# Top-k attention with an exact-GELU MLP on one core: larger halves before the reciprocal, one product copied before exponentials, two more items turned by squares

## The chip, the cores and the metric

The kernel runs on one core of a Trainium2 chip. The core has five engines that work side by side and meet through semaphores: TensorE (PE in the profile; its weight loads are listed apart as PEld), VectorE (DVE), ScalarE (ACT), GpSimd (POOL) and SyncE (SP), which here only issues DMAs. Each engine runs its own instructions strictly in the order in which the kernel wrote them; one that waits holds up all that stand behind it on the same engine. The metric is the device time of one execution in microseconds, as a median of several.

## The reference

All data are float32. The first half is attention that keeps the 32 largest scores of each row; the second is an MLP with an exact GELU on its output.

```python
B, H, S, D = 8, 8, 576, 64
scores = (q @ k.T) / sqrt(D)                     # per batch and head, 576 x 576
kth    = 32nd largest score of each row
scores = where(scores >= kth, scores, -1e9)
attn   = exp(scores - max); attn = attn / (sum(attn) + 1e-9)
x      = (attn @ v) reshaped to 4608 tokens x 512
out    = gelu(x @ w_in) @ w_out                  # w_in 512 x 2048, w_out 2048 x 512
```

## The kernel before, in words

**Items.** Attention is cut into 144 items. An item is a pair of heads of one batch and a tile of 128 query rows; its scores fill an SBUF tile `s` of 128 partitions by 2 x 576. The last 64 rows of the 576 are handled in items of their own, two head pairs together. A batch has 18 items, 16 of whole tiles and 2 of the last rows. Two batches, 36 items, repeat the same pattern; `RINGS` is 36, and "a ring" below means such a stretch. An item's place in its ring is its number modulo 36.

**The loop.** One loop over n writes the instructions of all engines by hand; it is the only thing that sets their order (`manual_schedule`). In step n it writes the scores of items n+2 and n+3 together when n is even (`scores`, L408 on TensorE, copied to `s` by ScalarE at L416, the keys of the last 64 columns at L381), the top-k of item n (`top_k`), mask and exponentials of item n-1 (`select` L538 and `softmax` L550 on ScalarE), the transposes of item n-2 (`transposes`), and the product with v of items n-3 or n-4 (`attend`, L742). Between these stand small pieces of the MLP (`mlp`): the first product (L811), GELU on ScalarE (L827) and the second product, which saves a multiplication by sums of blocks (L965 and L967; the sums of blocks are formed on GpSimd at L848 to L851). These pieces fill TensorE while attention waits for other engines.

**The top-k.** The row of 576 scores is split in two halves. Most items are "paired": VectorE writes the elementwise maximum of the halves into a tile `lists` (`larger`, L443), GpSimd writes their sum as integers (`sum_up`, L468) and later subtracts the maximum (`smaller`, L476), which leaves the smaller halves. VectorE then takes eight maxima at a time with MAX8 (L504) and MATCH_REPLACE8 (L507), first in the larger halves alone, then in all. Items 18 to 27 are not paired. After the last MAX8 of step n VectorE takes the reciprocal of item n-1's row sums (`inverse`, L525), for which GpSimd has added 1e-9 to the sums (`add_small`, L531). Behind them GpSimd writes the threshold and the exponent's bias of item n (`threshold`, L518 and L519), multiplies item n-1 by the reciprocals (`normalise`, L573) and starts `sum_up` for item n+2. `larger(n + 1)` is written at the head of step n, so on VectorE it stands right behind the reciprocal of step n-1. The tile `lists` has two buffers.

**From `s` to the product.** The product needs the probabilities with keys on the partitions. There are two ways. The first is on TensorE: one transpose for the last columns (L657) and eight for the others (L671) into PSUM, and ScalarE copies both to the tile `pt` (L660, L686). The second, "by squares" (`squared`), is off TensorE: VectorE transposes blocks of 32 by 32 inside `s` (`square_p`, L605, written in the middle of the next but one top-k), SP writes the result to DRAM (`write_p`, L615, four DMAs) and reads it back turned into `pt` (`read_p`, L625, four DMAs). Even items go by squares, and of the odd ones those whose place is in `LATER`; the latter are called "moved". The product of a moved item is written one step later, by `mids`, its PSUM tile is of the tag `pr`, which the transposes L671 and the second of two score tiles use too, and it is copied to `xT` by ScalarE (L747). The copy follows directly on the product in ScalarE's order; for a moved item it stands between the two exponentials of step n.

Of the kernel before, what the change touches and what calls it, by code (L numbers as in the profile page):

```python
# [14 lines left out]
def kernel(  # L15
# [19 lines left out]
    nc = tc.nc  # L35
    f32, i32, u32 = mybir.dt.float32, mybir.dt.int32, mybir.dt.uint32
    bf16, i16, u16 = mybir.dt.bfloat16, mybir.dt.int16, mybir.dt.uint16
    AF = mybir.ActivationFunctionType
    ALU = mybir.AluOpType

    B, H, S, D = q.shape
    P = 128
# [20 lines left out]
    work = ctx.enter_context(tc.tile_pool(name="work", bufs=2))  # L63
# [46 lines left out]
    def flush():  # L110
        held[0] = False
        while late_issues:
            late_issues.pop(0)()
        late_issues.extend(later)
        later.clear()
# [142 lines left out]
    for b in range(B):  # L258
# [4 lines left out]
        last = [(b * NP + p, NM) for p in range(0, NP, 2)]  # L263
# [13 lines left out]
    few = [False]  # L277
# [151 lines left out]
    lists_of = {}  # L429
    HS = S // 2  # L430

    def paired(i):

        return PAIRED <= i < N and i not in SINGLE

    def halves_of(i):
        s = S_of[i].rearrange("p (e h n) -> p e h n", e=2, h=2)
        return s[:, :, 0], s[:, :, 1]

    def larger(i):  # L440

        if paired(i):
            nc.vector.tensor_tensor(lists_of[i][:, :, 0], *halves_of(i), op=ALU.max)  # L443

    def into_of(i):

        if i < 2 and i not in into_lists:
            into_lists[i] = work.tile([P, 2, 2, HS], f32, tag="pt", bufs=1, name="into")
        return into_lists.get(i, lists_of[i])
# [3 lines left out]
    def first_lists():  # L453
# [6 lines left out]
        nc.gpsimd.tensor_tensor(both, a.bitcast(i32), top, op=ALU.subtract)  # L460
        nc.gpsimd.tensor_tensor(both, both, b.bitcast(i32), op=ALU.add)

    def sum_up(i):

        if paired(i):
            lists_of[i] = t = work.tile([P, 2, 2, HS], f32, tag="lists", name="lists")
            a, b = halves_of(i)
            nc.gpsimd.tensor_tensor(  # L468
                t[:, :, 1].bitcast(i32), a.bitcast(i32), b.bitcast(i32), op=ALU.add
            )  # L470
# [7 lines left out]
    def top_k(i, last, middle):  # L478


        stat_of[i] = st = {
            "first": work.tile([P, 2, 8], f32, tag="first", name="first"),
        }
        stat = work.tile([P, 4, 2], f32, tag="stat", name="stat")
        st.update((n, stat[:, x]) for x, n in enumerate(("neg", "bias", "den", "rden")))
        top = work.tile([P, 2, 16], f32, tag="top", bufs=1, name="top")
        into = [st["first"]] + [
            top[:, :, 8:16] if r == TOPK // 8 - 1 else top[:, :, 0:8] for r in range(1, TOPK // 8)
        ]
        if paired(i):  # L490
            t = lists_of[i]
            u = into_of(i)
            both = u.rearrange("p e h n -> p e (h n)")
            rounds = [(t[:, :, 0], u[:, :, 0]), (u[:, :, 0], u[:, :, 0])]
            rounds = [(*(rounds[r] if 16 * r < TOPK else (both, both)), x) for r, x in enumerate(into)]
        else:
            s = S_of[i].rearrange("p (e n) -> p e n", e=2)
            t = work.tile([P, 2, S], f32, tag="lists", name="rest")
            rounds = [(s if r == 0 else t, t, x) for r, x in enumerate(into)]
        for r, (src, dst, x) in enumerate(rounds):  # L500
            if 16 * r == TOPK:
                middle()
            for e in range(2):
                nc.vector.max(x[:, e], src[:, e])  # L504
            if r < len(rounds) - 1:
                for e in range(2):
                    nc.vector.match_replace(dst[:, e], x[:, e], src[:, e], LOWEST)  # L507
            if r == len(rounds) - 1:
                last()

        st["kth"] = top[:, :, 15]
# [9 lines left out]
    def inverse(i):  # L521
        if i < 0 or i >= N:
            return
        st = stat_of[i]
        nc.vector.reciprocal(st["rden"], st["den"])  # L525
# [17 lines left out]
    def softmax(i, e):  # L543

        if i < 0 or i >= N:
            return
        st, s = stat_of[i], row(i, e)
        if (i, e) not in selected:
            select(i, e)
        nc.scalar.activation(  # L550
            s, s, func=AF.Exp, bias=st["bias"][:, e : e + 1], scale=1.0,
            accum_out=st["den"][:, e : e + 1],
        )
# [23 lines left out]
    def squared(i):  # L577

        if not SINGLE.stop - 2 < i < N - 2:
            return False  # L580
        if items[i][1] == NM:
            return i % RINGS != RINGS // 2 - 1
        return moved(i) or (i % 2 == 0 and i % RINGS != 12)

    LATER = (3, 13, 25)

    def moved(i):

        return RINGS <= i < N - 8 and i % RINGS in LATER

    def delayed(i):

        return squared(i) and items[i][1] == NM
# [4 lines left out]
    RINGS = 2 * len(items) // B  # L598
    turned = {}

    def square_p(i):

        if squared(i):
            s = S_of[i]
            nc.vector.transpose(s, s)  # L605

    def write_p(i):

        if squared(i):
            turned[i] = d = dram.tile([SQ, NJ + NM, P // SQ, P], f32, tag="turned", name="turned")  # L610
            s = S_of.pop(i).rearrange("p (x j) -> p x j", j=SQ)
            d = d.rearrange("i c k n -> i (c k) n")
            for a in range(P // SQ):
                rows = slice(a * SQ, (a + 1) * SQ)
                nc.sync.dma_start(out=d[:, :, rows], in_=s[rows])  # L615
# [498 lines left out]
    def mlp(n):  # L1114
        for _ in range(n):
            if done[0] >= len(pieces) or pieces[done[0]][0] > ready[0] or left[0] == 0:
                return
            pieces[done[0]][1]()
            done[0] += 1
            left[0] -= 1  # L1120
            if eager[0]:
                run_gelus()
                run_small(9)
# [33 lines left out]
    for pair in range(2):  # L1157
        for piece in transpose_qk(pair, pair == 0):
            piece()
        if pair == 0:  # L1160
            scores(0)
            first_lists()
            scores(1)
            sum_up(1)
# [28 lines left out]
    starts_next = [x + 1 for x in starts]  # L1193
    sums_in = {START + 8 + j: j for j in range(FT // 2)}
    ahead = N + 4
    for n in range(ahead):

        held[0] = n < N and squared(n - 2)
        mid = [i for i in (n - 5, n - 4) if delayed(i) and n % 2 and (i % 2 or i in starts)]
        if moved(n - 4):  # L1200
            mid = [n - 4]
# [9 lines left out]
        def mids():  # L1211
            attend(mid.pop(0))
            if not mid:
                copy_x()
                read_p(n - 3)
                issue_soon()
# [7 lines left out]
        if n > 0:  # L1224
            larger(n + 1)
# [57 lines left out]
            softmax(n - 1, 1)  # L1283
        if few[0]:
            room = ODD if n % 2 else 0
            if mid and mid[0] in starts_next:
                mlp(1)
                mids()
                room -= 1
            if n % 2 or not ahead_of_x:  # L1290
                softmax(n - 1, 0)
            if mid:
                mlp(1)
                mids()
                room -= 1
            if n % 2 and ahead_of_x:
                softmax(n - 1, 1)
            mlp(room)
# [35 lines left out]
        mlp(left[0])  # L1334
        run_gelus()
        if n < N:
            top_k(n, lambda: inverse(n - 1), lambda: square_p(n - 2))
            write_p(n - 2)
            flush()
            if n == 0:  # L1340
                larger(1)
        else:
            inverse(n - 1)
        threshold(n)
        if n == 0:
            smaller(1)
        normalise(n - 1)
        sum_up(n + 2)
        if n in sums_in:
            weight_sums(sums_in[n])  # L1350
# [56 lines left out]
```

## Time and profile before

| | us |
|---|---|
| median of 3 runs (1465.57 to 1466.32) | 1465.61 |
| the profiled execution | 1466.12 |
| its span, first to last instruction | 1464.0 |
| TensorE busy | 1444.8 |
| VectorE busy | 1323.7 |
| GpSimd busy | 1138.0 |
| ScalarE busy | 1060.0 |

Rows of the timeline give the start in us from the span's beginning, the duration in us, the engine, the line of the kernel, the operation, the tiles as out<-in, the shapes, and how many were merged into the row. Square brackets hold the engine's idle time before it and who ended that. A matmul in float32 shows as two records. Rows of the groups give the count, busy us, the mean in ns, and the idle time before. Rows of the waits give the waiting instruction, the one that ended the wait, us in total, how often, and the longest. Rows of the windows give the window, its length, and each engine's busy us with its number of instructions (PE, PEld, DVE, ACT, POOL, as far as they are shown), then the granted share of TensorE's clock, the DMA share and GB/s. Rows of the DMAs end with the KB of one and the median us from issue to landing.

### The profile page before, as it was taken

To read this page: it belongs to the slowest core of one execution; us is meant where nothing else is said; L and a number is where in the kernel's file an instruction comes from. 1 tells how busy PE (TensorE), PEld (TensorE's weight loads), DVE (VectorE), ACT (ScalarE), POOL (GpSimd) and SP (SyncE) were. 2 spreads that over 40 slices of the span, in tenths; PEclk is the share of its full clock that TensorE was granted. 3 is DMA by queue.
4 is the path that set the end of the run, shared out by engine and by line. 5 is a ranking of instruction groups with operands and counts; after the bars stand their busy time and mean duration, and the time that the engine had idled before them with its cause. 6 is when DMAs were issued, how large, how long until landed. Compare 5 with 4: busy or idle time off the path is not lost. (4 is left out here: it accounts for less than half of the span.)

```text
span 1464.0 us, 26591 instructions
## 1 busy us (share of the span) xinstructions
PE 1444.8 (99%) x8639; PEld 1126.5 (77%) x8639; DVE 1323.7 (90%) x3337; ACT 1060.0 (72%) x1887; POOL 1138.0 (78%) x1290
## 2 busy tenths in 40 slices
PE   8999999999999999999999999999999999999999
PEld 6776677877777777787777778787777777787887
DVE  7999899999999999999999999999999999999701
ACT  7999977876777777767777777776776767677620
POOL 6877667877897879877898878887788887978632
PEclk9999999999999999999999999999999999999999
DMA  7524310045454446455454365455555443643300
GB/s 193 152 87 124 85 48 1 16 96 99 90 113 89 84 91 141 82 112 113 96 100 95 61 116 115 89 114 112 98 100 110 86 84 78 128 99 75 65 15 15
DMA packets 580043, 134.13 MB, mean 92 GB/s; under 512 B 494881, under 2 KB 571457, under 8 KB 579905
## 3 DMA queue, kind: packets, MB, share of 16 engines
q1 hardware_dynamic: 578640, 132.01, 42.6%
q8 instruction: 68, 1.11, 0.3%
q14 instruction: 71, 0.57, 0.1%
q10 hardware_dynamic: 1200, 0.39, 0.1%
q0 software_dynamic: 64, 0.03, 0.0%
HBM read 84.01 MB, written 48.37 MB: 90 GB/s over the span
## 5 line engine op out<-in xcount | busy, mean ns | idle before, releaser
L811 PE MATMUL h_ps<-xT,w_in_sb 128*128 128x256 f32 (+1 forms) x2560 | 533.2, 361 | 0.0
L811 PEld LDWEIGHTS h_ps<-xT,w_in_sb 128*128 128x128 f32 x2560 | 438.2, 190 | 70.3 <-issue 11.3
L504 DVE MAX8 top<-lists 128x8 f32<-128x576 f32 (+1 forms) x792 | 475.0, 638 | 0.0
L507 DVE MATCH_REPLACE8 lists<-top,lists 128x288 f32<-128x288 f32 (+1 forms) x528 | 307.4, 587 | 0.0
L538 ACT ACTIVATE s<-s,stat 128x576 f32<-128x576 f32 x288 | 217.8, 778 | 113.4 <-POOL stat L518 113.2
L573 POOL TENSOR_TENSOR s<-s,stat 128x1152 f32<-128x1152 f32 x135 | 286.3, 2121 | 0.3 <-DVE stat L525 0.3
L550 ACT ACTIVATE s<-s,stat 128x576 f32<-128x576 f32 x288 | 223.8, 780 | 7.6
L468 POOL TENSOR_TENSOR lists<-s 128x576 int32<-128x576 int32 x133 | 189.9, 1427 | 0.0
L476 POOL TENSOR_TENSOR lists<-lists 128x576 int32<-128x576 int32 x132 | 186.1, 1410 | 3.1
L742 PE MATMUL o<-pt,raw_v 128*64 128x256 f32 x1280 | 152.9, 384 | 1.5 <-issue 0.6
L416 ACT ACTIVATE s<-s_ps 128x1024 f32<-128x1024 f32 x127 | 125.0, 1032 | 39.6 <-PE s_ps L408 39.5
L531 POOL TENSOR_SCALAR stat<-stat 128x2 f32<-128x2 f32 x144 | 31.4, 218 | 153.7 <-ACT s L550 147.2
L742 PEld LDWEIGHTS o<-pt,raw_v 128*64 128x64 f32 x1280 | 87.4, 136 | 81.9 <-issue 38.9
L967 PE MATMUL y_ps<-w_out_sb,sum 128*128 128x256 f32 x472 | 140.4, 379 | 0.0
L408 PE MATMUL s_ps<-kt,qm 64*128 64x512 f32 x512 | 129.6, 619 | 0.8 <-ACT s L414 0.8
L827 ACT ACTIVATE g<-h_ps 128x512 f32<-128x512 f32 x144 | 78.2, 595 | 70.3 <-PE h_ps L811 69.7
L967 PE MATMUL y_ps<-w_out_sb,g 128*128 128x256 f32 x480 | 115.8, 381 | 0.0
L507 DVE MATCH_REPLACE8 lists<-first,lists 128x288 f32<-128x288 f32 x264 | 114.1, 437 | 0.0
L443 DVE TENSOR_TENSOR lists<-s 128x576 f32<-128x576 f32 x133 | 109.1, 821 | 4.4 <-ACT s L381 1.8
L504 DVE MAX8 first<-lists 128x8 f32<-128x288 f32 x268 | 106.3, 435 | 0.0
L967 PEld LDWEIGHTS y_ps<-w_out_sb,g 128*128 128x128 f32 x480 | 90.5, 190 | 14.4 <-issue 2.3
L967 PEld LDWEIGHTS y_ps<-w_out_sb,sum 128*128 128x128 f32 x472 | 89.7, 190 | 12.2
(162 smaller groups left out, 2373.4 us busy)
## 6 DMA issues: line engine op xcount, KB each, us to landing
turned<-s SPq DMA_DIRECT2D x264, 144.0 KB, 3.6
pt<-turned SPq DMA_DIRECT2D x264, 144.0 KB, 3.2
raw_v<-in_v_dram SPq DMA_DIRECT2D x64, 128.0 KB, 2.5
raw_q<-in_q_dram SPq DMA_DIRECT2D x112, 72.0 KB, 2.4
raw_k<-in_k_dram SPq DMA_DIRECT2D x112, 72.0 KB, 2.4
out_dram<-y SPq DMA_DIRECT2D x30, 256.0 KB, 3.1
w_out_sb<-in_moe_w_in_dram SPq DMA_DIRECT2D x14, 511.8 KB, 4.9
w_out_sb<-in_moe_w_out_dram SPq DMA_DIRECT2D x10, 511.8 KB, 4.0
```

The lines of the kernel that those rows point to most:

```text
L408: nc.tensor.matmul(s_ps[:, e], lhsT=q_t[rows, :], rhs=kt[rows, main_keys(pair)], start=True, stop=True)
L416: nc.scalar.activation(spread(s, S + TL, SM), s_ps, func=AF.Copy, scale=scale)
L468: nc.gpsimd.tensor_tensor(t[:, :, 1].bitcast(i32), a.bitcast(i32), b.bitcast(i32), op=ALU.add)
L476: nc.gpsimd.tensor_tensor(into_of(i)[:, :, 1].bitcast(i32), both, top, op=ALU.subtract)
L504: nc.vector.max(x[:, e], src[:, e])
L507: nc.vector.match_replace(dst[:, e], x[:, e], src[:, e], LOWEST)
L538: nc.scalar.activation(s, s, func=AF.Prelu, bias=st["neg"][:, e : e + 1], scale=1.0, alpha=STEEP)
L550: nc.scalar.activation(s, s, func=AF.Exp, bias=st["bias"][:, e : e + 1], scale=1.0, accum_out=st["den"][:, e : e + 1],)
L573: nc.gpsimd.tensor_tensor(s, s, wide, op=ALU.mult)
L742: nc.tensor.matmul(o[e * D : (e + 1) * D, 0:n], lhsT=vt[:, j, e, :], rhs=pt[:, e * NJ + j if j < NM else NM, :], start=(j == 0), stop=(j = ...
L811: nc.tensor.matmul(h_tile(u)[:, i, :], lhsT=w_in_sb[:, ko, f * P : (f + 1) * P], rhs=xT[:, ko, c0 : c0 + n], start=(ko == 0), stop=(ko == ...
L967: nc.tensor.matmul(acc[names][:, k], lhsT=lhsT, rhs=rhs, start=(j == 0 and k == 0), stop=(j == FT // 2 - 1 and k == 1),)
```

## The change

Three edits. First, from step 13 on, `larger(n + 2)` is written inside `top_k(n)`, after the last MAX8 and before the reciprocal, instead of at the head of step n+1, behind the reciprocal; the tile `lists` is taken there by whoever comes first. Second, the moved product of place 3 of a ring (items 39, 75 and 111) is written, with its copy to `xT`, before the first of the step's two exponentials instead of between the two. On TensorE the order does not change by it. Third, place 31 joins `LATER`: items 67 and 103 go by squares, and their products are written one step later. On TensorE their nine transposes go, the scores that followed them are written earlier, and the ten matmuls of each product stand behind sixteen of the first MLP product instead of before them.

```diff
+    have_larger = set()
+
     def larger(i):
-        if paired(i):
-            nc.vector.tensor_tensor(lists_of[i][:, :, 0], *halves_of(i), op=ALU.max)
+        if paired(i) and i not in have_larger:
+            have_larger.add(i)
+            nc.vector.tensor_tensor(lists_for(i)[:, :, 0], *halves_of(i), op=ALU.max)
...
+    def lists_for(i):
+        if i not in lists_of:
+            lists_of[i] = work.tile([P, 2, 2, HS], f32, tag="lists", name="lists")
+        return lists_of[i]
+
     def sum_up(i):
         if paired(i):
-            lists_of[i] = t = work.tile([P, 2, 2, HS], f32, tag="lists", name="lists")
+            t = lists_for(i)
...
-    LATER = (3, 13, 25)
+    LATER = (3, 13, 25, 31)
...
             room = ODD if n % 2 else 0
-            if mid and mid[0] in starts_next:
+            if mid and (mid[0] in starts_next or mid[0] % RINGS == LATER[0]):
                 mlp(1)
                 mids()
                 room -= 1
...
-            top_k(n, lambda: inverse(n - 1), lambda: square_p(n - 2))
+            def last():
+                if few[0]:
+                    larger(n + 2)
+                inverse(n - 1)
+
+            top_k(n, last, lambda: square_p(n - 2))
```

## The prediction

> **What bounds the kernel now.** I read the head of the page first, then the busy time in long windows, the waits, and last the timeline where a wait of TensorE is named.
>
> ```profile
> span 1464.0 us, 26591 instructions
> ...
> PE 1444.8 (99%) x8639; PEld 1126.5 (77%) x8639; DVE 1323.7 (90%) x3337; ACT 1060.0 (72%) x1887; POOL 1138.0 (78%) x1290
> ```
> ```profile
> 362.00:706.00 344.00, 342.30 (x2025) 267.21 (x2024) 331.30 (x838) 250.56 (x452) 285.83 (x323) 1.00 0.51 101
> ```
>
> The second row is one stretch of 344 us, about 36 items (a ring, below). TensorE is busy in 342.30 of it and VectorE in 331.30, so TensorE sets the pace, but VectorE has only 13 us to spare in 36 items, 0.35 an item. Work taken from TensorE shortens the run only as far as the others can follow. Who waits for whom:
>
> ```profile
> ACT s L538 <- POOL stat L518: 113.2, 43, 6.1
> ...
> DVE stat L525 <- POOL stat L531: 55.2, 68, 6.2
> ...
> PE tp L671 <- ACT xT L747: 2.9, 3, 1.0
> ```
>
> TensorE has one large wait, three times 1.0 us, for the copy of a product into xT. ScalarE waits 113.2 us for the threshold (L518), which stands behind the top-k on VectorE. VectorE's wait at the reciprocal is 55.2 us in 68 of 144 items, 0.81 each. One of the three waits of TensorE, in the timeline:
>
> ```profile
> 418.29 0.74 DVE L504 MAX8 top<-lists 128x8 f32<-128x576 f32 x1
> ...
> 418.99 0.22 POOL L531 TENSOR_SCALAR stat<-stat 128x2 f32<-128x2 f32 x1
> 419.24 0.17 DVE L525 RECIPROCAL stat<-stat 128x2 f32<-128x2 f32 x1 [0.21 <-POOL stat L531]
> 419.29 0.22 POOL L518 TENSOR_SCALAR stat<-top 128x2 f32<-128x2 f32 x1
> ...
> 419.47 0.67 POOL L519 TENSOR_TENSOR stat<-top,first 128x2 f32<-128x2 f32 x1
> 419.54 1.44 ACT L538 ACTIVATE s<-s,stat 128x576 f32<-128x576 f32 x2 [6.11 <-POOL stat L518]
> ...
> 419.56 2.38 PE L742 MATMUL o<-pt,raw_v 128*64 128x256 f32 x20
> ...
> 423.26 0.59 PE L967 MATMUL y_ps<-w_out_sb,sum 128*128 128x256 f32 x2
> 423.26 0.38 ACT L986 COPY p<-seven 128x256 f32<-128x256 f32 x1
> ...
> 423.70 0.49 PE L373 MATMUL tp_t<-kt,qm 128*128 128x128 f32 x2
> ...
> 424.02 0.27 PE L657 MATMUL tp_t<-ident,s 128*128 128x128 f32 x1
> ...
> 424.13 0.60 PE L967 MATMUL y_ps<-w_sum,sum 128*128 128x256 f32 x2
> ...
> 424.56 0.59 PE L967 MATMUL y_ps<-w_out_sb,sum 128*128 128x256 f32 x2
> ...
> 424.96 0.77 ACT L550 ACTIVATE s<-s,stat 128x576 f32<-128x576 f32 x1
> ...
> 425.73 0.35 ACT L747 COPY xT<-o 128x256 f32<-128x256 f32 x1
> ...
> 426.13 1.09 PE L671 MATMUL tp<-ident,s 128*128 128x128 f32 x8 [0.97 <-ACT xT L747]
> ...
> 427.06 0.60 PE L967 MATMUL y_ps<-w_sum,g 128*128 128x256 f32 x2
> ```
>
> The product (L742) ends at 421.94. ScalarE, held until 419.54 by the threshold, comes to its copy only at 425.73, behind a table load and one exponential (0.77). The transposes L671 want the same PSUM tile. The pair before them runs from 424.56, and pairs stand 0.43 apart (424.13 to 424.56), so L671 could have started at 424.99. It starts at 426.13: 1.14 us lost.
>
> **The change, part by part.**
>
> *The copy ahead of the exponentials* (item 3 of each ring from the second on: three places, those of the wait row). The copy then follows L986, which ends at 423.64, takes 0.35 and is done at 424.0, a microsecond before 424.99. The stall of 1.14 goes, three times: 3.42 us on TensorE. ScalarE does the same work in another order, so the second exponential ends when it did. Bounds: 0 and 3.42.
>
> *Two odd items by squares* (items 67 and 103). TensorE loses in each eight transposes (426.13 to 427.06, 0.93) and one (424.02 to 424.13, 0.11): 1.04 an item, 2.08 in all. What comes in its place:
>
> ```profile
> L605 DVE STREAM_TRANSPOSE s<-s 128x1152 f32<-128x1152 f32 x66 | 89.9, 1362 | 0.0
> ```
> ```profile
> L686 ACT COPY pt<-tp 128x1024 f32<-128x1024 f32 x67 | 68.3, 1020 | 38.8 <-PE tp L671 37.8
> ```
> ```profile
> pt<-turned SPq DMA_DIRECT2D x264, 144.0 KB, 3.2
> ```
>
> VectorE gets 1.36 an item, ScalarE loses a copy of 1.02 and a small one. SP issues eight more DMAs an item. They go ahead of a load of keys, and the loads of v now stand behind the later product; those values are used in the next pair of batches, so I cost the queue at nothing, and 3.2 us if a product comes to wait for its landing. The product itself moves some 8 us later on TensorE, with no change of its time. Its copy is put between two exponentials, as that of item 3 was, so the stall just removed can return here, at most 1.14 each. I expect 0.4: ScalarE's copy is about as late as TensorE is early. Left: 0.6 an item; bounds 1.04 and -0.1.
>
> *The larger halves ahead of the reciprocal.* Nothing is added; L443 and L525 change places in nearly every item after the twelfth. Three effects, none on TensorE itself.
>
> ```profile
> 685.35 0.20 POOL L519 TENSOR_TENSOR stat<-top,first 128x2 f32<-128x2 f32 x1
> ...
> 685.50 2.11 POOL L573 TENSOR_TENSOR s<-s,stat 128x1152 f32<-128x1152 f32 x1
> ...
> 685.77 2.45 DVE L443 TENSOR_TENSOR lists<-s 128x576 f32<-128x576 f32 x1 [0.62 <-ACT s L381]
> ...
> 687.57 1.93 POOL L468 TENSOR_TENSOR lists<-s 128x576 int32<-128x576 int32 x1
> ```
> ```profile
> 341.90:344.60 2.70, 2.48 (x1) 1.00 0.73 144
> ...
> 1343.70:1346.50 2.80, 2.66 (x1) 1.00 0.01 3
> ```
>
> First, a gain. The second block is VectorE's time in L443 alone. Four times (342, 686, 1030, 1344; the first and the last stand here) it takes some 2.5 us instead of 0.76. At 685.77 it starts 0.27 after the normalising L573 has started on GpSimd and ends 0.62 after that has ended, while GpSimd's next one, L468, takes 1.93. The two engines shut each other out. With the new order L573 waits for a reciprocal that stands behind L443, so this collision cannot happen: 1.7 us of VectorE back, four times. (At the second and third of them the added square of 1.36 stands a few microseconds ahead and takes most of it.)
>
> Second, a loss. The same exclusion now falls on the threshold.
>
> ```profile
> 27.00 0.71 POOL L518 TENSOR_SCALAR stat<-top 128x2 f32<-128x2 f32 x1 [0.29 <-DVE stat L525]
> ```
> ```profile
> 26.90 0.74 DVE L443 TENSOR_TENSOR lists<-s 128x576 f32<-128x576 f32 x1
> ```
>
> Here L518 came 0.1 after L443 had started, and took 0.71 instead of 0.22: it ended when L443 did. In the timeline at 419, MAX8 ends at 419.03; L443 now starts at about 419.1, before L518 at 419.29, and holds it to some 419.95, where it ended at 419.51. So the threshold ends about 0.45 later wherever VectorE and GpSimd arrive together, and what ScalarE does behind it (419.54) too. L519 afterwards takes 0.20 (685.35) and not 0.67, so the normalising is not later. The Trainium skill, in "SBUF — State Buffer", section "Who interferes with whom", states this as a rule: a VectorE instruction with two SBUF inputs and a GpSimd instruction that reads SBUF exclude each other, and whichever issues first holds the port for its whole length. The rows above agree with it; it speaks against this part of the change.
>
> Third, small: a reciprocal takes 0.08 of VectorE's time when it is not hidden (457.56 to 457.64, below). The 76 that did not wait are now bare, about 19 a ring, 1.5 us. The 68 that waited 0.81 can get up to a whole L443 (0.76) back, where what they wait for is not itself shut out by L443.
>
> *What the others give back.* TensorE can run ahead only until another chain holds it. The nearest places are the same in every ring. At 423.70 tp_t waits for the same bank as L986, which ends at 423.64: no margin. And some 40 us on:
>
> ```profile
> 457.56 0.17 DVE L525 RECIPROCAL stat<-stat 128x2 f32<-128x2 f32 x1 [1.65 <-POOL stat L531]
> ...
> 457.64 0.76 DVE L443 TENSOR_TENSOR lists<-s 128x576 f32<-128x576 f32 x1
> ...
> 457.86 1.44 ACT L538 ACTIVATE s<-s,stat 128x576 f32<-128x576 f32 x2 [3.41 <-POOL stat L518]
> ...
> 466.17 1.06 ACT L686 COPY pt<-tp 128x1024 f32<-128x1024 f32 x1
> ...
> 466.50 1.99 PE L408 MATMUL s_ps<-kt,qm 64*128 64x512 f32 x8
> ...
> 468.41 2.38 PE L742 MATMUL o<-pt,raw_v 128*64 128x256 f32 x20
> ```
>
> The copy L686 ends at 467.23; the second item's scores (half of 466.50 to 468.41 on, 467.46) need its tile: margin 0.23. ScalarE is held by the threshold until 457.86 here and has no long pause after it. So TensorE may be ahead by 0.23 plus what the threshold gains.
>
> In the ring from 362, VectorE comes 1.7 earlier from the collision at 342, less 0.08 for some eight items: 1.0 to 1.1. Less 0.45 for the threshold, about 0.65; 0.23 and 0.65 let 0.9 of the 1.14 pass. In the two later rings the square takes 1.36 of 1.7 plus 0.62 (the wait at 685.77): 0.9 left, 0.3 after the reciprocals, and nothing or less after the 0.45; 0.2 to 0.6 of 0.6 and 1.14 passes, I take 0.45. Sum by this: 0.9 + 0.45 + 0.45 = 1.8 us. If nothing held TensorE it were 3.42 + 2.08 = 5.5. The place at 467 is one reading, and the threshold there came late through GpSimd (VectorE, waiting for the same engine, stood for 1.65 at 457.56), which the first effect also brings forward; so I take 2.6, nearer to the chain than to the free sum. 1466.12 - 2.6 = 1463.5 on the profiled execution. The median before, 1465.61, lies 0.51 below that execution, so 1463.0.
>
> **Rivals.**
> - *Everything passes* (0.22): the 68 waits of 0.81 shrink, ScalarE follows, no place holds TensorE. Gain 4 to 5.5: 1460.1 to 1461.6. For it: 37.8 and more of ScalarE's waits are for TensorE itself. Against: the margins of 0 and 0.23.
> - *The copies and squares change nothing* (0.13): the stall moves to the next tight place, gain below 0.8, down to -0.8: 1464.8 to 1466.4. For it the 0.45 of the threshold in front of a margin of 0.
> - *Slower* (0.10): the excluded threshold becomes the bound. Place: every ring's four tight spots, each pays 0.45 less its margin, some 0.4, 0.25, 0.25, 0.4: 1.3 a ring, 3.9 in three, and the squares' 1.36 twice in a stretch where VectorE has no pause, 2.7. Against the 2.08 and nothing else saved: +4.5, 1470.1. It decides where VectorE's gain from the collisions (1.7 a ring) falls below 0.45 plus the bare reciprocals. The rule of "SBUF — State Buffer" in the Trainium skill would give this if the exclusion hit all even items alike.
>
> **How the numbers follow.** The likeliest, part of it kept (0.55), gives a gain of 0.8 to 4.0: 1461.6 to 1464.8, and I forecast 1463.0. 0.2%, 2.9 us, is about what a measurement of this kernel can tell from no change; the forecast lies just inside. Two fifths of the likeliest case lie above 2.9: faster 0.22 + 0.22 = 0.44; same 0.33 + 0.13 = 0.46; slower 0.10. The range 1459.9 to 1466.4 holds all but the slower case and a few hundredths.
>
> **What would show it.** The wait of tp L671 for xT L747 three times near 1 us is gone, or two shorter ones stand where the products of items 67 and 103 are copied. L443 has no instance above 2 us. L518's mean rises and L519's falls. VectorE's wait at L525 falls from 55.2. L671 counts 16 fewer. The prediction is wrong if TensorE's waits in a ring are below 0.5 us (then all passes), or if new waits for L986 and L686 sum to more than 5 us (slower), or if a product waits for its DMA.

## The result and the profile after

The changed kernel takes 1461.65 us in the median of 8 runs (1461.13 to 1462.52), the kernel before 1465.86 (1464.96 to 1467.45) in the same comparison: a ratio of 0.9970, 95% interval 0.9959 to 0.9981. That is 4.2 us less, above the 0.2% (2.9 us) that the prediction set for "faster", 1.35 us below its 1463.0 and inside its range. Head of the page after:

```profile
span 1459.5 us, 26550 instructions
...
PE 1442.6 (99%) x8621; PEld 1123.9 (77%) x8621; DVE 1329.6 (91%) x3339; ACT 1056.4 (72%) x1883; POOL 1128.4 (77%) x1290
```

These views answer to those shown of before. The groups after:

```profile
L446 DVE TENSOR_TENSOR lists<-s 128x576 f32<-128x576 f32 x133 | 106.2, 799 | 17.8 <-ACT s L381 5.8 <-DVE top L513 0.9
...
L680 PE MATMUL tp<-ident,s 128*128 128x128 f32 x536 | 69.6, 273 | 0.0
...
L528 POOL TENSOR_TENSOR stat<-top,first 128x2 f32<-128x2 f32 x144 | 55.9, 388 | 0.0
L527 POOL TENSOR_SCALAR stat<-top 128x2 f32<-128x2 f32 x144 | 45.5, 316 | 64.3 <-DVE top L513 40.3 <-DVE stat L534 9.8 <-DMA turned<-s 5.3
```

The names have moved by some lines: L443 is now L446, L518 is L527, L519 is L528, L525 is L534, L531 is L540, L671 is L680, L686 is L695, L747 is L756. There are 16 transposes L680 fewer, and they wait for nothing; before, three of them waited 2.9 us. The threshold's mean went from 264 ns (38.1 us in 144) to 316, the bias's from 586 to 388. The waits after, and under them one row of the same view of before:

```profile
ACT s L547 <- POOL stat L527: 122.9, 45, 6.2
...
DVE stat L534 <- POOL stat L540: 27.8, 27, 6.2
...
PEld s_ps L408 <- ACT pt L695: 9.1, 20, 1.0
```
```profile
PEld s_ps L408 <- ACT pt L686: 6.1, 17, 0.8
```

VectorE's wait at the reciprocal has halved (55.2 before), but 13 us of the 27 turned up one instruction earlier, as idle time before L446 (17.8 us, 4.4 before). VectorE waits there instead, so that part was no gain. And one wait of TensorE has grown, its weight load for the scores L408 behind the copy L695. This wait became the centre of the study. Two timelines of the changed kernel show the wait that is gone and the one that came:

```profile
423.29 0.38 ACT L995 COPY p<-seven 128x256 f32<-128x256 f32 x1
...
423.54 0.41 ACT L756 COPY xT<-o 128x256 f32<-128x256 f32 x1
...
423.96 1.28 ACT L559 ACT_TABLE_LOAD   x1
...
425.02 1.04 PE L680 MATMUL tp<-ident,s 128*128 128x128 f32 x8
...
454.64 1.42 POOL L485 TENSOR_TENSOR lists<-lists 128x576 int32<-128x576 int32 x1
455.90 0.78 DVE L446 TENSOR_TENSOR lists<-s 128x576 f32<-128x576 f32 x1
456.15 0.61 POOL L540 TENSOR_SCALAR stat<-stat 128x2 f32<-128x2 f32 x1
456.79 0.17 DVE L534 RECIPROCAL stat<-stat 128x2 f32<-128x2 f32 x1
456.83 0.22 POOL L527 TENSOR_SCALAR stat<-top 128x2 f32<-128x2 f32 x1
...
465.33 2.31 PE L408 MATMUL s_ps<-kt,qm 64*128 64x512 f32 x8
465.39 1.06 ACT L695 COPY pt<-tp 128x1024 f32<-128x1024 f32 x1
...
466.50 0.30 PEld L408 LDWEIGHTS s_ps<-kt,qm 64*128 64x128 f32 x4 [0.87 <-ACT pt L695]
```

At 423 the product's copy (L756) stands ahead of the table load and is done at 423.95; the transposes start at 425.02 without a wait. At 455.90 VectorE, now ahead of GpSimd, starts L446, and GpSimd's small L540 takes 0.61 instead of 0.22. The threshold L527 follows it, ScalarE follows the threshold, and ten microseconds later TensorE's weight load for the second item's scores waits for ScalarE's copy L695 (0.87 us; 0.48 at this place before). The matmuls behind it take 2.31 us instead of 1.99, so 0.32 us of TensorE's own time goes there.

### The profile page after: what moved, and what is told of

It reads as the page before. It is cut to its first block, busy times and chain, and to the rows that moved or that the text cites. A ratio compares the mean times of both kernels' runs of the same rounds, so it can differ in the third digit from the quotient of the medians.

```text
span 1459.5 us, 26550 instructions
## 1 busy us (share of the span) xinstructions
PE 1442.6 (99%) x8621; PEld 1123.9 (77%) x8621; DVE 1329.6 (91%) x3339; ACT 1056.4 (72%) x1883; POOL 1128.4 (77%) x1290
## 4 chain that ended last, share of the span: by engine, by line
PE 44%; POOL 11%; DVE 7%; issue 3%; ACT 3%; DMA 1%; SPq 0%; DVEq 0%; POOLq 0%; ACTq 0%
PE h_ps L820 17%; PE y_ps L976 11%; PE o L751 5%; PE s_ps L408 3%; POOL s L582 3%; DVE top L513 3%; DVE lists L516 2%; POOL lists L485 2%; POOL lists L477 2%; PE seven L974 2%; PE tp L680 2%; PE y_ps L938 2%; PE y_ps L941 1%; DMA turned<-s 1%; DVE s L614 1%
## 5 line engine op out<-in xcount | busy, mean ns | idle before, releaser
L540 POOL TENSOR_SCALAR stat<-stat 128x2 f32<-128x2 f32 x144 | 44.4, 309 | 163.0 <-ACT s L559 156.1
L751 PEld LDWEIGHTS o<-pt,raw_v 128*64 128x64 f32 x1280 | 86.8, 136 | 80.9 <-issue 38.1
L408 PE MATMUL s_ps<-kt,qm 64*128 64x512 f32 x512 | 131.2, 621 | 1.1 <-ACT s L414 0.8
L446 DVE TENSOR_TENSOR lists<-s 128x576 f32<-128x576 f32 x133 | 106.2, 799 | 17.8 <-ACT s L381 5.8
```

What stands on the lines that cost most here:

```text
L408: nc.tensor.matmul(s_ps[:, e], lhsT=q_t[rows, :], rhs=kt[rows, main_keys(pair)], start=True, stop=True)
L751: nc.tensor.matmul(o[e * D : (e + 1) * D, 0:n], lhsT=vt[:, j, e, :], rhs=pt[:, e * NJ + j if j < NM else NM, :], start=(j == 0), stop=(j = ...
```

## The experiments

All times are medians, with the interval of the ratio to the kernel before of the same comparison (its median 1466.05 to 1466.22 us). In the texts below, e1 to e11 are the runs by the number that their names begin with. "Steps 2, 6 and 10" are those whose n leaves 2, 6 or 10 when divided by 36; 424 and 457 lie in steps 6 and 10 of the second ring, 381 in step 2.

### The three edits apart

**Without the new order on VectorE.**

```diff
             def last():
-                if few[0]:
-                    larger(n + 2)
                 inverse(n - 1)
```

> The copy ahead of the exponentials and the two more items by squares, without the larger halves ahead of the reciprocal (L446 behind L534 again). Theory A (the new order of VectorE is needed: its 1.7 us at step 34 of each ring pay for the squares, and two pauses of some 0.4 to 0.5 us at steps 2 and 10 are its price): the squares of 1.36 us are no longer paid, TensorE waits again behind a late threshold in the second and third ring, and 1463.0 to 1464.3 us come out, 1.4 to 2.7 above the changed kernel. Rival B (TensorE alone decides: 3.42 of stalls and 2.08 of transposes, whatever VectorE does): as the changed kernel or, without the exclusions at steps 2 and 10, up to 2.5 better, 1459.2 to 1461.7 us. The collisions of some 2.5 us at L446 are back in both.

Measured: 1460.59 us (1460.38 to 1460.93, 5 runs), ratio 0.9963 (0.9949 to 0.9976). Rival B, and theory A is wrong. The gain is 5.46 us; the sum of TensorE's own savings was 3.42 + 2.08 = 5.50. All five runs lie below all eight of the changed kernel.

The two sums agree more closely than their parts do. TensorE's lead on the kernel before (read as in the table further down) ends at 5.14 us in the trace of this run. Of that, 0.37 is there before any edit acts, when both kernels still run the same instructions; 3.54 comes at the three copies, 0.95 at items 67 and 103, and 0.28 elsewhere, mainly where the kernel before waits for a DMA.

**The new order alone.** `LATER` is (3, 13, 25) and the condition for the early copy is the old one; the rest is the changed kernel:

```diff
-    LATER = (3, 13, 25, 31)
+    LATER = (3, 13, 25)
...
-            if mid and (mid[0] in starts_next or mid[0] % RINGS == LATER[0]):
+            if mid and mid[0] in starts_next:
```

> Only the larger halves ahead of the reciprocal. Theory A: VectorE's lead of 1.7 us a ring meets the three stalls of TensorE for the copy of xT, which stay at 1.0 to 1.2 us, and nothing passes; at steps 2 and 10 the stalls are taken from that wait: 1465.2 to 1466.0 us, no change. Rival C (the new order gains by itself, through VectorE's shorter wait at the reciprocal): 1463.0 to 1464.5 us. Rival D (the excluded threshold costs by itself): above 1466.5 us.

Measured: 1468.18 us (1467.26 to 1468.49, 11 runs), ratio 1.0014 (1.0005 to 1.0022): 2.1 us slower, rival D.

**Each of the two other edits alone.** The first pair of lines just shown, with the old order on VectorE, is `e5_copy_alone`; the second pair, likewise, is `e6_squares_alone`.

> Only the copy of item 3's product ahead of the exponentials. Theory F (the chain to the tight places comes back to TensorE, through the expert sums on GpSimd that wait for TensorE's products, so that it moves with TensorE and the three stalls of 1.14 us go in full): 1466.05 - 3.42 = 1462.6 us, between 1462.2 and 1463.0, no new wait at 424 and 467, where the margins stay at 0 and 0.23. Theory G (the prediction's: the places at 424 and 467 hold TensorE by the clock): 0.23 to 0.9 of each stall passes, 1463.4 to 1465.4 us.

> Only items 67 and 103 by squares; the three stalls of 1.14 us remain. Theory F: 2.08 us of transposes pass in full, VectorE's two more squares of 1.36 us cost nothing: 1464.0 us, between 1463.5 and 1464.4. Theory H (VectorE has no pause there, and the square or a stall of some 0.4 for the copy comes back on TensorE): 1464.6 to 1466.0 us.

Measured: the copy alone 1462.32 us (10 runs), ratio 0.9976 (0.9966 to 0.9985), a gain of 3.9; the squares alone 1464.50 us (11 runs), ratio 0.9990 (0.9981 to 0.9999), a gain of 1.7. Theory F for the copy. In its trace TensorE's lead rises by 1.2 us at each of the three copies (0.16 to 1.35, 1.37 to 2.56, 2.71 to 3.91) and is unchanged past 467 and past the same place of the other rings; nothing there took any of it back. The squares end between the bounds of F and H. Their gain of 1.7 has an interval of 0.1 to 2.8, and in their trace the lead rises by 0.66 over item 67 and by 0.02 over item 103. By medians the two sum to 5.6, what they bring together (5.5). The timeline of `e1_copy_and_squares` shows why the copies pass whole:

```profile
450.72 0.73 POOL L857 TENSOR_TENSOR sum<-g 128x256 f32<-128x256 f32 x1 [0.91 <-PE y_ps L976]
...
454.27 1.40 POOL L485 TENSOR_TENSOR lists<-lists 128x576 int32<-128x576 int32 x1
455.75 0.22 POOL L540 TENSOR_SCALAR stat<-stat 128x2 f32<-128x2 f32 x1
...
456.05 0.22 POOL L527 TENSOR_SCALAR stat<-top 128x2 f32<-128x2 f32 x1
456.30 1.44 ACT L547 ACTIVATE s<-s,stat 128x576 f32<-128x576 f32 x2 [3.40 <-POOL stat L527]
...
464.61 1.06 ACT L695 COPY pt<-tp 128x1024 f32<-128x1024 f32 x1
...
464.94 1.99 PE L408 MATMUL s_ps<-kt,qm 64*128 64x512 f32 x8
...
465.72 0.38 PEld L408 LDWEIGHTS s_ps<-kt,qm 64*128 64x128 f32 x4 [0.47 <-ACT pt L695]
```

and the same place in the kernel before:

```profile
452.27 0.73 POOL L848 TENSOR_TENSOR sum<-g 128x256 f32<-128x256 f32 x1 [2.10 <-PE y_ps L967]
...
455.83 1.40 POOL L476 TENSOR_TENSOR lists<-lists 128x576 int32<-128x576 int32 x1
457.31 0.22 POOL L531 TENSOR_SCALAR stat<-stat 128x2 f32<-128x2 f32 x1
```

GpSimd's run up to the threshold starts with a sum that waits for a product of TensorE (the bracket), and goes on from there without a break. Where TensorE is early, the whole chain is early: L540 stands 5.04 us behind the start of the first sum before, and 5.03 without the new order; the copy L695 starts 1.56 us earlier (466.17, now 464.61), as much as TensorE. The margin that the prediction read as 0.23 travels with it: the matmuls take 1.99 us, as before.

### Where the new order costs

**The old order at steps 2 and 10, then at 2, 6 and 10, then the new one at these alone.**

```diff
-                if few[0]:
+                if few[0] and n % RINGS not in (2, 10):
                     larger(n + 2)
```

(`not in (2, 6, 10)` in the second, `in (2, 6, 10)` in the third.)

> The changed kernel, with the old order of L446 and L534 at steps 2 and 10 of each ring alone. Theory A: TensorE's six waits of 0.20 to 0.30 us at the scores (L408) for the copy L695, and with them what TensorE gives back there (0.38 to 0.5 each by the shift of the two traces, 2.4 us in all), go or shrink: 1459.0 to 1460.2 us. Rival E (VectorE or ScalarE is late at those places for another reason than the port): 1461.3 to 1462.2 us, with the six waits still there.

Measured: 1461.96 us (1461.39 to 1463.51, 8 runs), ratio 0.9973 (0.9963 to 0.9983). Neither: the six waits are gone, and the time is not better. The timeline has a new wait at step 6:

```profile
419.04 0.22 POOL L540 TENSOR_SCALAR stat<-stat 128x2 f32<-128x2 f32 x1
419.07 0.76 DVE L446 TENSOR_TENSOR lists<-s 128x576 f32<-128x576 f32 x1
419.33 0.58 POOL L527 TENSOR_SCALAR stat<-top 128x2 f32<-128x2 f32 x1
...
424.10 0.49 PE L373 MATMUL tp_t<-kt,qm 128*128 128x128 f32 x2 [0.24 <-ACT p L995]
```

Here L446 holds the threshold itself, 0.58 instead of 0.22, and TensorE is 0.41 late at 424.10, and so at 766.98 and 1109.55. In the changed kernel this wait does not show; TensorE has fallen back by 0.4 at step 2 by then (the table below).

> The changed kernel with the old order of L446 and L534 at steps 2, 6 and 10 of each ring. Theory I (the cost of the new order lies at the few steps where the threshold or GpSimd's sums, held by L446, stand on the chain back to TensorE; in e3_not_at_2_and_10 the wait went to step 6, three times 0.41 us at 424, 767 and 1110): these waits go too, 1460.4 to 1461.0 us, level with e1_copy_and_squares. Rival J (the cost is spread, and moves on to a fourth place): 1461.3 to 1462.2 us.

> The changed kernel with the new order of L446 and L534 at steps 2, 6 and 10 of each ring alone, the counterpart of e7_not_at_2_6_10. Theory I (the whole cost of the new order lies at these steps): level with the changed kernel, 1461.4 to 1462.3 us, with waits of 0.2 to 0.3 us at the scores six times. Rival J (the cost needs the new order elsewhere too): 1460.4 to 1461.0 us, level with e1_copy_and_squares.

Measured: 1460.56 us (1460.30 to 1461.71, 5 runs), ratio 0.9965 (0.9951 to 0.9978), without the three steps; 1462.39 us (1461.84 to 1462.65, 8 runs), ratio 0.9973 (0.9962 to 0.9984), with them alone. Theory I, the second 0.1 above its bound: all eight runs of the second lie above all five of the first. Three steps in a ring of 36 carry the whole cost, and the new order everywhere else is worth nothing. One row of the waits says the same. In this order: `e1_copy_and_squares`, `e7_not_at_2_6_10`, `e9_only_2_6_10`.

```profile
PEld s_ps L408 <- ACT pt L695: 6.8, 20, 0.8
```
```profile
PEld s_ps L408 <- ACT pt L695: 6.7, 20, 0.8
```
```profile
PEld s_ps L408 <- ACT pt L695: 8.9, 19, 0.9
```

Against 9.1 in the changed kernel the difference is 2.3 us, six places of 0.39. That is idle time of the weight loads; the matmuls lose 0.32 of it at the place shown above.

**The new order at step 34 alone**, where the collision of 2.45 us had been: `if few[0] and n % RINGS == 34`.

> The changed kernel, with the new order of L446 and L534 at step 34 of each ring alone (where the collision of 2.45 us stood), the old one elsewhere. Theory A: the collision is all that the new order gives to the sum: as e3_not_at_2_and_10 within 0.5 us, 1459.0 to 1460.4. Rival C (the shorter waits at the reciprocal in the other steps carry some of it): 1461.0 to 1463.5 us, above the changed kernel or level with it, and more waits of TensorE behind the threshold.

Measured: 1460.64 us (1460.40 to 1461.29, 5 runs), ratio 0.9965 (0.9952 to 0.9977). That is above theory A's bounds and below rival C's, and level with no new order at all (1460.59). The run takes away one collision only: without the new order L446 takes 2.48 us at 341.62 and 2.20 at 1349.5, while near 686 and 1030, behind the added squares, it takes no longer than elsewhere; with it at step 34 the first is gone. The new order alone is the wider test. There all four collisions are gone (no L446 above 1.63 us), and TensorE's lead on the kernel before, which has them, is the same on both sides of each: -0.03 us at 342, -0.51 at 686, -1.33 at 1030, -2.06 at 1344. The collisions that the prediction took for a gain of 1.7 us a ring cost TensorE nothing.

A table shows where TensorE's lead on the kernel before goes. It is read off an instruction that follows TensorE closely, ScalarE's copy of the last keys (L381), by its end in each trace, in us:

| step n (place) | before at | lead, changed | lead, e1 | lead, e9 |
|---|---|---|---|---|
| 38 (2) | 378.71 | 0.34 | 0.37 | 0.22 |
| 40 (4) | 398.38 | -0.09 | 0.37 | -0.11 |
| 44 (8) | 436.50 | 1.17 | 1.55 | 1.19 |
| 48 (12) | 474.12 | 0.86 | 1.56 | 0.87 |
| 72 (0) | 704.55 | 1.99 | 2.43 | 1.39 |
| 76 (4) | 742.16 | 1.68 | 2.43 | 1.07 |
| 80 (8) | 780.29 | 2.96 | 3.61 | 2.31 |
| 84 (12) | 817.90 | 2.65 | 3.60 | 2.00 |
| 136 (28) | 1312.57 | 4.21 | 5.14 | 3.57 |

The copy ahead of the exponentials gives 1.2 to 1.3 each time (from place 4 to 8). The changed kernel loses 0.3 to 0.4 on either side of it, 2.0 us at the six places together, e1 nothing. Between 48 and 72 the changed kernel gains 0.3 on e1, part of it at a product near 526 that starts 0.2 late in e1 and not in the changed kernel. e9, as late as the changed kernel at 48, falls 0.6 behind it by 72; there the product at 687.50 starts 0.45 late. The kernel before waits at such products too (0.26 us at 526.39, 0.63 at 870.54; none there after). What decides these waits is not shown. So part of the 2.0 us comes back, and 1.1 us are left against e1 (1461.65 and 1460.59).

### GpSimd on the way back to TensorE

Four small additions of zero on GpSimd behind `add_small`, with the old order on VectorE, at a step where GpSimd runs without a break and at one where it waits for VectorE:

```diff
         add_small(n - 1)
+        if few[0] and n % RINGS == 10:
+            for _ in range(4):
+                den = stat_of[n - 1]["den"]
+                nc.gpsimd.tensor_scalar(den, den, 0.0, None, op0=ALU.add)
```

(`== 30` in the second.)

> As e1_copy_and_squares, with four more small instructions on GpSimd (as L540, adding zero) between the sum's small addition and the threshold at step 10 of each ring: the threshold some 0.75 us later, with no change of VectorE's order. Theory F (GpSimd stands there on the chain back to TensorE, with about 0.2 us to spare): 0.5 to 0.8 us lost in each of three rings, 1462.0 to 1463.0 us, with a wait of TensorE for the copy L695 near 466, 807 and 1149. Rival L (the cost of the new order comes from VectorE and not through GpSimd): 1460.3 to 1461.0 us.

> The same four instructions at step 30 of each ring, where GpSimd has done the small addition 2.7 us before the top-k on VectorE ends and then waits for it. Theory F: hidden, level with e1_copy_and_squares, 1460.3 to 1461.0 us. Rival M (any lengthening of GpSimd's work costs, 1138 us busy of 1459): as e10_extra_at_10.

Measured: at step 10 1464.55 us (11 runs), ratio 0.9988 (0.9979 to 0.9997); at step 30 1461.60 us (6 runs), ratio 0.9969 (0.9958 to 0.9981). Rivals L and M fall: the same instructions cost 4.0 us at one place and 1.0 at the other. Both are above what theory F gave. At step 10 the additions (L1338) delayed the threshold by more than I had worked out; each takes 0.22, but they start 0.30 apart:

```profile
456.41 0.22 POOL L540 TENSOR_SCALAR stat<-stat 128x2 f32<-128x2 f32 x1
456.71 1.11 POOL L1338 TENSOR_SCALAR stat<-stat 128x2 f32<-128x2 f32 x4
457.78 0.22 POOL L527 TENSOR_SCALAR stat<-top 128x2 f32<-128x2 f32 x1
```

From L540 to L527 it is 1.37 us, against 0.30 in e1 (455.75 to 456.05): 1.07 more, and TensorE's lead falls by 1.0 from step 44 to 48 and in the two later rings (0.92 to -0.10, 0.58 to -0.42, 1.65 to 0.65), 3.0 in all. Past a margin of some 0.1 the loss is one to one. At step 30 GpSimd still has a wait for VectorE behind the four:

```profile
645.01 1.10 POOL L1338 TENSOR_SCALAR stat<-stat 128x2 f32<-128x2 f32 x4
647.70 0.22 POOL L527 TENSOR_SCALAR stat<-top 128x2 f32<-128x2 f32 x1 [1.59 <-DVE stat L534]
```

TensorE's lead does not change there (0.71 on both sides in the second ring, 3.22 in the third). So at the step itself they are hidden, as theory F has it. What that trace has is a wait for a DMA at another place:

```profile
525.66 2.38 PE L751 MATMUL o<-pt,raw_v 128*64 128x256 f32 x20 [0.93 <-DMA pt<-turned]
```

In e1 the same product starts 0.2 late, in the changed kernel it does not wait, in `e4_only_at_34` it waits 1.0 us, and in the run with the additions at step 10, at 527.36, also 1.0, about what its 4.0 has beyond the 3.0. These runs do not explain that spread, and so what the 1.0 us by medians of the run at step 30 come from stays open.

### One more item by squares

`LATER = (3, 13, 25, 31, 21)`, on `e1_copy_and_squares`.

> As e1_copy_and_squares, and item 21 of each ring from the second on (57, 93, 129) by squares as well: three times 1.04 us of transposes less on TensorE, three squares of 1.36 us more on VectorE, where it waits 1.06 us at the reciprocal two steps on. Theory F: 1460.6 - 3.1 = 1457.5 us, between 1457.1 and 1458.4. Rival K (VectorE, the copy of the moved product or its DMA holds TensorE in its place): 1459.5 to 1462.5 us, with a new wait for xT, or for pt by DMA, at steps 24 and 25.

Measured: 1467.86 us (11 runs), ratio 1.0011 (1.0002 to 1.0019), 7.3 us above e1 and outside both. Rival K named the waits, but not their size:

```profile
592.80 2.38 PE L751 MATMUL o<-pt,raw_v 128*64 128x256 f32 x20 [1.79 <-DMA pt<-turned]
```
```profile
694.51 0.35 ACT L756 COPY xT<-o 128x256 f32<-128x256 f32 x1
694.76 0.78 ACT L559 ACTIVATE s<-s,stat 128x576 f32<-128x576 f32 x1
694.91 0.86 PEld L680 LDWEIGHTS tp<-ident,s 128*128 128x128 f32 x8 [1.37 <-ACT xT L756]
```

The product of the new item waits 1.8 us for its data from DRAM, and the copy between two exponentials now stalls the transposes at 694.91 (item 67), too. The new items' products wait 1.79, 0.52 and 2.11 us for their data in the three rings, and the transposes wait for such a copy four times, 3.5 us. The prediction had put 0.4 on this stall. In the changed kernel the same copy (691.79, 0.35) ends 0.1 us before the transposes start (692.24).

## Why the prediction was right or wrong

**The copy ahead of the exponentials: right.** The three waits for xT are gone, 3.42 was the size (3.9 by the medians of the run alone, three times 1.2 in its trace), and it was taken in full.

**Two items by squares: right that they pay, too high in the size of 1.04 an item.** The stall of 0.4 at the copy did not come, by 0.1 us. But TensorE's lead rises by 0.78 over item 67 and by 0.38 over item 103 in the changed kernel, by 0.79 and 0.16 in e1. At item 103 the product starts late; in the changed kernel:

```profile
1029.29 1.95 PE L751 MATMUL o<-pt,raw_v 128*64 128x256 f32 x16 [0.34 <-issue]
```

The row names nobody. The four reads of its data were issued from 1023.74 to 1026.28 and take 3.2 us to land by the median, so the DMA that I had costed at nothing is the likely cause, not a shown one. Why item 67 gives 0.8 and not 1.04 is open. That VectorE's squares of 1.36 us cost TensorE anything shows in no run.

**The larger halves ahead of the reciprocal: the places right, the account wrong.** The collisions are gone (no L446 above 1.64 us), the bias is shorter, and the threshold is later by what I had said (0.45; 0.36 and 0.39 in the rows above). But I entered VectorE's 1.7 us a ring as a gain, and set the late threshold off against it. Neither belongs there: the new order alone takes all four collisions away and TensorE's lead does not move at any of them, and the threshold is paid by TensorE directly. The rule in the Trainium skill, "SBUF — State Buffer", section "Who interferes with whom", that whichever of the two issues first holds the port, agrees with both directions (L540 0.61 behind L446, and before, L443 2.45 behind L573). What it cannot say is which of these 0.4 us count: here those at three steps of 36.

**The step that failed** is "What the others give back": "So TensorE may be ahead by 0.23 plus what the threshold gains." I read the places at 424 and 467 as fixed in time, because ScalarE stood there waiting for the threshold and GpSimd was late. I did not ask what GpSimd had been waiting for. Its row at 452.27 names TensorE. A margin in a chain that comes back to the engine itself is no limit to a gain of that engine: it limits only how much longer the chain may become. The forecast gave back 2.9 of 5.5. Of the three stalls nothing is given back (1.2 each in the trace of the copy alone), and without the new order the kernel gains 5.46 by medians. With it, 1.3 are missing (5.5 - 4.2), and the cause is not the one that the sum gives: the chain became longer by 0.4 at places with some 0.1 to spare (0.41 longer at 457, and 0.32 lost in the matmuls at 466), so the 0.23 was too large a margin as well. The forecast came within 1.4 us by luck: a loss that does not exist (2.9) stood in for one that does (1.3).

**The rivals.** "Everything passes" holds for the copy. Of the 2.08 us of the squares 1.7 pass by medians and about half in the traces (0.95 in e1, 1.16 in the changed kernel). "Slower" described the real mechanism of the first edit (the excluded threshold at each ring's tight spots); alone that edit is 2.1 us slower. What I had set as the sign, new waits summing to more than 5 us, was too coarse: 2.3 us in one row carried it.

The version without the new order, 1460.59 us, is level with the two that keep it away from the three steps (1460.56 and 1460.64); no run was faster than these.

## What to carry to other kernels

Before a tight place is taken for a limit, follow its chain back past the engine that is late, to what that engine waited for: if it ends at the engine that you are speeding up, the place moves along. Conversely, time put into another engine inside such a loop counts past a small margin (here 1.0 of 1.07 us), though that engine is idle a quarter of the time. And a shorter wait on an engine that is not the bound is no gain until someone who waits for it is named.

## What was not expected

GpSimd's addition on 128 by 2 elements takes 0.22 us, but four more of them on the same tile make the way to the threshold 1.07 us longer. The same four take 1.0 us of TensorE's lead in each ring at one step and none at another. Moving one VectorE instruction of 0.76 us past one of 0.15, with no work added, costs 2.1 us.
